# A fixed table of engine sequences, x[128] as a rank-1 term on VectorE, and GpSimd sums, in a Fourier and two-layer feed-forward kernel

## The chip, the cores and the metric

The kernel runs on one core of a Trainium2 chip. The metric is the device time of one execution in microseconds (us). A core has five engines that matter here: TensorE (PE in the profile, matrix products into the PSUM banks), VectorE (DVE), ScalarE (ACT), GpSimd (POOL) and SyncE (SP, which issues most DMA transfers). Each engine executes its own instructions strictly in the order in which they stand in its program, and waits at an instruction until the semaphores that it needs have been raised.

## What the kernel computes

The reference takes the real part of a two-dimensional Fourier transform and feeds it through two feed-forward layers:

```python
X = np.fft.fft(np.fft.fft(x, axis=1), axis=2).real       # x: 2 x 3008 x 256
x = X.reshape(6016, 256)
r = np.maximum(x @ w_in, 0.0)                             # layer 1: 256 -> 2048 -> 256
x = (r * r) @ w_out
h = x @ w_in2                                             # layer 2: 256 -> 2048 -> 256
P = a[0] + a[1]*h + a[2]*h*h + a[3]*h*h*h
Q = 1.0 + abs(b[0])*abs(h) + abs(b[1])*h*h
out = (P / (Q + 1e-6)) @ w_out2
```

The products need float32 accuracy. Each operand is therefore split into a rounded high part and a low rest, and a product is three matmuls: high by high, low by high and high by low.

## The kernel before, in words

The 6016 tokens are cut into 12 tiles: tile 0 has 384 tokens, tiles 1 to 11 have 512 (`TILES`, in units of 128). The 2048 hidden features are 16 chunks of 128. The Fourier transform along the sequence is done once for all tokens at the start (`u_mm`, `u_copy`, `u_out`, into `U`), and U for tiles 2 to 11 is spilled to DRAM. The transform along the 256 columns is done tile by tile: `fm` (matmuls, `f_d`), `fv` (copy on ScalarE), `fs` (matmuls, `f_s`), `fe` and `ff` (high and low part, `x1h` and `x1l`). The same tile's two halves of tokens are mirror images, so that from tile 2 on (tiles that are not in `DIRECT`) layer 1 multiplies an even and an odd half of 256 columns each, and gets the tokens as sum and difference of the two products.

Layer 1 on one chunk of such a tile is this chain of operations: `h1` on PE (`h1_mm`, into one PSUM bank); `b1` on ACT, which copies the odd half to SBUF; `s1` and `s2` on DVE, sum and difference into the 512-column buffer `g` (`e1_s`); `r1`, `a1`, `i1` on ACT (relu, square rounded, square); `c1` on POOL (the low part, `e1_lo`); `o1` on PE (6 matmuls of 512 columns). There are 160 such chunks (10 tiles by 16). Column 128 of the transformed input, x[128], belongs to neither half; `h1` adds it with a seventh matmul per chunk, whose stationary operand is the weight row `w0` in an otherwise empty 128 by 128 matrix and whose moving operand is `X0`, the rows that `q_row` loads from `qdram`.

Layer 2 runs on 23 subtiles: tile 0, and two of 256 tokens for each other tile. A group (two chunks of a 256-token subtile, 512 columns; one chunk of 384 in tile 0) is: `h2` (PE, 12 matmuls of 256 columns); `u` = |b1||h| and `t1` on ACT; `q` = (u + |b0|) h, `t2` and `t3` on DVE; `w` = |q|, `y` and `z` on ACT (z is 1/Q); `gh`, `m`, `e` on DVE; `c2` on POOL (`e2_gl`); `o2` on PE (12 matmuls of 256 columns). So there are 16 groups in a 512-token tile. The last two subtiles have another form (`ALONE`: `gh` on POOL; `FIN`: two single chunks).

The order of every engine is made when the program is built. `Queues.run` is a list scheduler: it holds a cost for every operation and a `place`, and takes again and again the operation that can start earliest, ties by place; `SHIFT` moves places of groups of operations. Buffers are counted in `SLOTS` (a buffer, such as `g` with two, is taken by one operation and given back by a later one), and so are the PSUM banks: `p0` to `p3`, `o1a`, `o1b`, `o2a`, `o2b`. Before, `h1` and `h2` take one of p0, p1, p2, o2b, and `m` writes p3. Loads and stores stand in one queue on SP, in program order; a store of output waits there for its ACT copy.

The lines that matter: L743 (`h1`'s matmuls) and L745 (the seventh), L769 (`o1`, `o2`), L713 (`h2`), L788 (`s1`, `s2`), L813 (`c1`), L842 (`q`), L850 (`t2`), L854 (`t3`), L876 (`gh`), L882 (`m`), L889 (`e`), L893 (`c2`), L911 and L912 (output).

Of the kernel before, what the change touches and what calls it, by code (L numbers as in the profile page):

```python
# [9 lines left out]
F32 = mybir.dt.float32  # L10
# [20 lines left out]
SLOTS = dict(xt=4, x1h=2, x1l=2, x0=2, x2h=2, x2l=2, ut=1, v=2, g=2, bc=2, g1=2, u=4, t1=4, y=3, g2=3, os=1,  # L31
# [36 lines left out]


def ranks(key):  # L70

# [41 lines left out]
}


class Queues:
# [19 lines left out]
    def run(self):  # L136
        waits, users = {}, {}
# [6 lines left out]
        ready = {}  # L144
        for op in self.ops:
            ready.setdefault(op["engine"], [])
            if not waits[op["n"]]:
                ready[op["engine"]].append(op)
        clock = dict.fromkeys(ready, 0.0)
        order = []  # L150
        while any(ready.values()):
            best = None
            for e, ops in ready.items():
                now = clock[e]
                for op in ops:
                    start = max(now, op["at"], self.port if op["port"] else 0.0)
                    for tag in op["take"]:
                        at = self.first(tag)[0]
                        if at is None:
                            break  # L160
                        start = max(start, at)
                    else:
                        rank = (start, op["place"], op["n"])
                        if best is None or rank < best[0]:
                            best = rank, op
            (start, _, _), op = best
# [5 lines left out]
            end = start + op["cost"]  # L172
# [954 lines left out]
```

## Time and profile before

| | |
|---|---|
| median of three runs | 1049.68 us (1049.3 to 1049.74) |
| the profiled execution | 1048.59 us |
| its span, first to last instruction | 1046.6 us |
| mean granted TensorE clock | 0.998 |
| PE, PEld busy | 1021.6 us (98%), 968.4 us (93%) |
| DVE, ACT, POOL busy | 998.0 us (95%), 955.6 us (91%), 495.0 us (47%) |
| matmuls | 7538 |

PEld is the loading of weights into the array, beside the matmuls. An instruction's duration in the profile runs to the end of its last write, and the next instruction of the same engine may start before that; so the time that an instruction takes of its engine is better read from the distance of two starts than from its duration, and the busy time of PE, DVE and ACT is an upper bound of their work.

### The profile page before, as it was taken

Reading aid. Unit: us, or ns where it says so; the run is one execution under the profiler, and the core shown is the slowest. Engines: PE = TensorE matmul, PEld = TensorE weight load, DVE = VectorE, ACT = ScalarE, POOL = GpSimd, SP = SyncE. Lnnn points to the kernel's source line nnn. Section 1 sums busy time; section 2 is a strip of 40 time slices with the busy share of each in tenths; the row PEclk is TensorE's granted clock in tenths of the full one; section 3 lists DMA queues with packets and bytes.
Section 4 is the critical chain, followed back from the end, with each engine's and each line's share of the span. In section 5 each row is a group of like instructions: output and inputs, shape, how many; then the busy total and the mean of one; then the engine's idle time right before and its main releaser. Section 6 shows DMA issues by size and latency. Waiting matters only on the chain.

```text
span 1046.6 us, 20738 instructions
## 1 busy us (share of the span) xinstructions
PE 1021.6 (98%) x7538; PEld 968.4 (93%) x7538; DVE 998.0 (95%) x1789; ACT 955.6 (91%) x1921; POOL 495.0 (47%) x373
## 2 busy tenths in 40 slices
PE   9899989999999999999999999999999999999986
PEld 9889989999999999999999999999999999999985
DVE  6999999999999999999999799999999999999998
ACT  3688989999998999999999899999899989999896
POOL 0000026545555555455555645655564545555476
PEclk9999999999999999999999999999999999999999
DMA  9653500000000000000000000000000000000000
GB/s 350 215 204 111 169 1 1 9 19 12 11 12 11 12 19 3 12 11 12 11 12 11 1 11 22 1 12 16 16 11 11 2 11 12 2 11 11 1 12 21
DMA packets 26939, 36.90 MB, mean 35 GB/s; under 512 B 2349, under 2 KB 19445, under 8 KB 26837
## 3 DMA queue, kind: packets, MB, share of 16 engines
q1 hardware_dynamic: 26725, 35.19, 9.9%
q8 instruction: 59, 0.97, 0.4%
q14 instruction: 43, 0.35, 0.1%
q10 hardware_dynamic: 112, 0.39, 0.1%
HBM read 26.74 MB, written 8.80 MB: 34 GB/s over the span
## 4 chain that ended last, share of the span: by engine, by line
PE 76%; DVE 9%; ACT 9%; DMA 3%; issue 2%; POOL 1%; POOLq 0%; SPq 0%; ACTq 0%; DVEq 0%
PE o2a L769 20%; PE p L713 15%; PE o1a L769 10%; PE o1b L769 10%; PE p L743 8%; PE o2b L713 5%; PE o2b L743 2%; PE p L745 1%; DMA g<-in_dram 1%; DVE g L876 1%; DMA xt<-in_dram 1%; PE o2b L769 1%; DVE p L882 1%; ACT t L836 1%; DVE t L854 1%
## 5 line engine op out<-in xcount | busy, mean ns | idle before, releaser
L893 POOL TENSOR_TENSOR g<-t,y 128x512 fp32r<-128x512 f32 (+1 forms) x182 | 250.5, 1376 | 248.7 <-DVE t L889 182.2
L813 POOL TENSOR_TENSOR g<-g,g 128x512 fp32r<-128x512 f32 x160 | 216.3, 1353 | 285.9 <-ACT g L808 237.0
L769 PE MATMUL o2a<-g,w2hi 128*128 128x256 f32 (+1 forms) x1440 | 258.7, 280 | 6.3 <-POOL g L893 6.3
L769 PEld LDWEIGHTS o2a<-g,w2hi 128*128 128x128 f32 x1440 | 209.2, 188 | 12.6 <-POOL g L893 7.9
L769 PE MATMUL o2a<-g,w2lo 128*128 128x256 f32 (+1 forms) x720 | 143.6, 279 | 0.0
L876 DVE SCALAR_TENSOR_TENSOR g<-t,ab,y 128x512 fp32r<-128x512 f32 (+1 forms) x176 | 136.8, 780 | 4.6 <-ACT y L863 2.8
L769 PE MATMUL o1a<-g,w1hi 128*128 128x512 f32 x352 | 139.5, 396 | 0.0
L769 PE MATMUL o1b<-g,w1hi 128*128 128x512 f32 x352 | 138.3, 393 | 0.0
L882 DVE SCALAR_TENSOR_TENSOR p<-u,g 128x512 f32<-128x512 f32 (+1 forms) x176 | 132.0, 750 | 0.1
L889 DVE SCALAR_TENSOR_TENSOR t<-t,ab,p 128x512 f32<-128x512 f32 (+1 forms) x176 | 127.5, 724 | 0.3
L863 ACT ACTIVATE y<-y 128x512 f32<-128x512 f32 (+1 forms) x185 | 117.8, 637 | 1.2
L713 PE MATMUL p<-x2h,w2hi 128*128 128x256 f32 (+1 forms) x540 | 109.7, 284 | 7.3 <-DVE x1h L887 2.5
L846 ACT ACTIVATE u<-u 128x512 f32<-128x512 f32 (+1 forms) x176 | 110.3, 628 | 6.5 <-DVE u L842 6.1
L788 DVE TENSOR_TENSOR g<-p,bc 128x256 f32<-128x256 f32 x260 | 106.0, 414 | 9.7 <-POOL g L813 7.6
L804 ACT ACTIVATE g<-g 128x512 fp32r<-128x512 f32 (+1 forms) x175 | 110.1, 630 | 5.1 <-PE o1b L769 4.5
L798 ACT ACTIVATE g<-g 128x512 f32<-128x512 f32 x160 | 101.8, 637 | 13.7 <-DVE g L788 13.2
L859 ACT ACTIVATE y<-u 128x512 f32<-128x512 f32 (+1 forms) x176 | 110.9, 631 | 1.9
L808 ACT ACTIVATE g<-g 128x512 f32<-128x512 f32 (+1 forms) x175 | 110.2, 631 | 1.0
L769 PEld LDWEIGHTS o2a<-g,w2lo 128*128 128x128 f32 x720 | 109.8, 188 | 0.0
L713 PE MATMUL p<-x2h,w2lo 128*128 128x256 f32 (+1 forms) x540 | 108.3, 282 | 0.0
L713 PE MATMUL p<-x2l,w2hi 128*128 128x256 f32 (+1 forms) x540 | 108.1, 282 | 0.0
L842 DVE SCALAR_TENSOR_TENSOR u<-u,ab,p 128x512 f32<-128x512 f32 (+1 forms) x134 | 96.8, 723 | 6.1 <-ACT t L836 5.5
(265 smaller groups left out, 2768.4 us busy)
## 6 DMA issues: line engine op xcount, KB each, us to landing
g<-in_dram SPq DMA_DIRECT2D x48, 256.0 KB
xt<-in_dram SPq DMA_DIRECT2D x15, 384.0 KB
out_dram<-os SPq DMA_DIRECT2D x22, 256.0 KB
udram<-U SPq DMA_DIRECT2D x4, 640.0 KB
ut<-udram SPq DMA_DIRECT2D x10, 256.0 KB
x2h<-in_dram SPq DMA_DIRECT2D x8, 256.0 KB
x2l<-in_dram SPq DMA_DIRECT2D x8, 256.0 KB
x<-qdram SPq DMA_DIRECT2D x30, 1.0 KB
```

The lines of the kernel that those rows point to most:

```text
L713: nc.tensor.matmul(h[:, c * n:(c + 1) * n], l[:, k, :], r[:, k], start=(q == 0), stop=(q == 5))
L769: nc.tensor.matmul(O[t][e], l[:, e * 128:(e + 1) * 128], r[:, c * n:(c + 1) * n], start=(i == 0 and q == 0 and (e == 0 or not one)), stop= ...
L804: nc.scalar.activation(out=e["gh"], in_=e["g"], func=ACTF.Square)
L808: nc.scalar.activation(out=e["g"], in_=e["g"], func=ACTF.Square)
L813: eng.tensor_tensor(out=e["gl"], in0=e["g"], in1=f32(e["gh"]), op=ALU.subtract)
L846: nc.scalar.activation(out=w, in_=w, func=ACTF.Abs)
L859: nc.scalar.activation(out=e["z"], in_=e["w"], func=ACTF.Abs_reciprocal_sqrt, bias=Q1)
L863: nc.scalar.activation(out=z, in_=z, func=ACTF.Square)
L876: nc.vector.scalar_tensor_tensor(out=e["gh"], in0=e["t1"], scalar=a0, in1=e["z"], op0=ALU.add, op1=ALU.mult)
L882: nc.vector.scalar_tensor_tensor(out=e["m"], in0=e["w"], scalar=Q1, in1=f32(e["gh"]), op0=ALU.add, op1=ALU.mult)
L889: nc.vector.scalar_tensor_tensor(out=e["t1"], in0=e["t1"], scalar=a0, in1=e["m"], op0=ALU.add, op1=ALU.subtract)
L893: (nc.vector if (t, j) in FIN else nc.gpsimd).tensor_tensor(out=e["gl"], in0=e["t1"], in1=e["z"], op=ALU.mult)
```

## The change

It has three parts. First, `SHIFT` and the `place` of each operation go; a table `ORDER` gives each of the five engines its whole sequence, and `Queues.run` only deals out buffers and banks in that order. With it `bc` has 3 buffers, `u` and `t1` 5, `y` 4, and p3 joins the banks of `h1` and `h2`.

Second, in tiles 2 to 11 the seventh matmul goes. x[128] now stands in row 64 of the odd half (`q_row`, now step `fq`: two DMA rows into `x1h` and `x1l` after `ff`), so that the sum `s1` holds it; the difference needs a correction, which `s2` adds as `beta` (a weight column per chunk) times `X0` (a row that `q_wide` broadcasts to all partitions) in one scalar_tensor_tensor on DVE, and POOL subtracts the odd half in a new step `s3`. The zeroing, placing and rounding of the 128 by 2048 matrix `w0` go, and the load of w_in's row moves behind the first 16 weight chunks.

Third, for groups in `SUMS` (j % 4 == 1: 40 groups of 512 columns and 4 of 384) the sum |b0||h| + |b1|h² is no longer made on DVE by `q`: ACT makes |b0||h| (`u`) and the square (`v`), and POOL adds them (`w`). In the other groups `q` writes into the h2 bank, and so does `m` (p3 is no longer needed); `t3` of `SUMS` writes into the bank instead. There `m` takes its first operand from SBUF, and in the others from the bank.

```diff
-SLOTS = dict(xt=4, x1h=2, x1l=2, x0=2, x2h=2, x2l=2, ut=1, v=2, g=2, bc=2, g1=2, u=4, t1=4, y=3, g2=3, os=1,
+SLOTS = dict(xt=4, x1h=2, x1l=2, x0=2, x2h=2, x2l=2, ut=1, v=2, g=2, bc=3, g1=2, u=5, t1=5, y=4, g2=3, os=1,
...
-BANKS5 = BANKS + ("o2b",)
+BANKS5 = BANKS + ("o2b", "p3")
...
+ORDER = dict(
+    SP=
+    "040I06050J08070K090A0L0B0C0M03000N010O0P020Q0R0S0T0U0V0o0W0X0H0p0Y0D0F0E0Z0G0z0a1J0b0c0d0e0f0g0h0i0j"
...
+        for e, text in ORDER.items():
+            place = [62 * DIGITS.index(a) + DIGITS.index(b) for a, b in zip(text[::2], text[1::2])]
...
+    SUMS = [(t, j) for t in range(M) for j in range(len(GROUPS2[t])) if (t, j) not in ALONE + FIN and j % 4 == 1]
...
+    def q_wide(t):
+        X0[t] = x0t[t % 2]
+        nc.sync.dma_start(out=X0[t], in_=q_part(t, 2).partition_broadcast(128))
+
     def q_row(t):
...
+        for part in range(2):
+            nc.sync.dma_start(out=f32(X1[t][part][64:65, 1, :]), in_=q_part(t, part).unsqueeze(0))
...
+            if k == jobs[-1] and t not in DIRECT:
+                add(("fq", t), "SP", 0.2, lambda t=t: q_row(t), needs=["qd"] + [("ff", t, i) for i in jobs], lat=DMA_LAT)
...
-            for b in range(2):
-                for q, (l, r) in enumerate(((wh, xh), (wl, xh), (wh, xl))):
-                    nc.tensor.matmul(h[:, b, c], l[:, b, :], r[:, b, :n], start=(q == 0), stop=(b == 1 and q == 2))
-                if b == 0:
-                    nc.tensor.matmul(h[:, 0, c], w0[:, i], X0[t][:, :n], start=False, stop=True)
+            for q, (l, r) in enumerate(((wh, xh), (wl, xh), (wh, xl))):
+                for b in range(2):
+                    nc.tensor.matmul(h[:, b, c], l[:, b, :], r[:, b, :n], start=(c + q + b == 0), stop=(c == gs - 1 and q == 2 and b == 1))
...
+        if part == 0:
+            nc.vector.tensor_tensor(out=g[:, 0], in0=H1[t, j][:, 0, 0], in1=b, op=ALU.add)
+        elif part == 1:
+            i = GROUPS1[t][j][0]
+            nc.vector.scalar_tensor_tensor(out=g[:, 1], in0=X0[t], scalar=beta[:, i:i + 1], in1=H1.pop((t, j))[:, 0, 0],
+                                           op0=ALU.mult, op1=ALU.add)
+        else:
+            nc.gpsimd.tensor_tensor(out=g[:, 1], in0=g[:, 1], in1=b, op=ALU.subtract)
...
+    def e2_v(t, j):
+        e = E2[t, j]
+        e["z"] = sb(tag2("y", t, j), [128, NMAX])[:, :e["n"]]
+        nc.scalar.activation(out=e["z"], in_=H2[t, j], func=ACTF.Square, scale=SCALES[3])
+
+    def e2_vw(t, j):
+        e = E2[t, j]
+        nc.gpsimd.tensor_tensor(out=e["w"], in0=e["w"], in1=e["z"], op=ALU.add)
...
-        e["w"] = H2[t, j] if (t, j) in ALONE + FIN else w
+        e["w"] = H2[t, j]
         nc.vector.scalar_tensor_tensor(out=e["w"], in0=w, scalar=b0, in1=H2[t, j], op0=ALU.add, op1=ALU.mult)
...
+        e["t3"] = H2[t, j] if (t, j) in SUMS else e["t1"]
+        nc.vector.scalar_tensor_tensor(out=e["t3"], in0=e["t1"], scalar=a1, in1=H2[t, j], op0=ALU.add, op1=ALU.mult)
...
-        e["m"] = e["w"] if (t, j) in ALONE + FIN else ps(tag2("m", t, j), [128, NMAX])[:, :e["n"]]
+        e["m"] = e["w"]
         nc.vector.scalar_tensor_tensor(out=e["m"], in0=e["w"], scalar=Q1, in1=f32(e["gh"]), op0=ALU.add, op1=ALU.mult)
```

Three places show what that makes of the programs. On TensorE, this is a chunk of `h1` of tile 7 before (p_7580 is its bank, x1h and x1l the two parts of its input, w_73 the matrix with the row of x[128]):

```order
L743 MATMUL p_7580<-x1h,w1hi_78 128x256
L743 MATMUL p_7580<-x1h,w1lo_94 128x256
L743 MATMUL p_7580<-x1l,w1hi_78 128x256
L745 MATMUL p_7580<-x_75,w_73 128x256
L743 MATMUL p_7580<-x1h,w1hi_78 128x256
L743 MATMUL p_7580<-x1h,w1lo_94 128x256
L743 MATMUL p_7580<-x1l,w1hi_78 128x256
```

In the changed kernel the same step reads as follows, and the six matmuls of `o1` of an earlier chunk come behind it:

```order
L788 MATMUL p_7483<-x1h,w1hi_78 128x256 x2
L788 MATMUL p_7483<-x1h,w1lo_94 128x256 x2
L788 MATMUL p_7483<-x1l,w1hi_78 128x256 x2
L812 MATMUL o1a<-g_7417,w1hi_91 128x512
L812 MATMUL o1b<-g_7417,w1hi_91 128x512
```

Seven matmuls have become six; the even and the odd half alternate, and nothing that needs `X0` is left on TensorE.

On VectorE, in the middle of tile 6, these are consecutive instructions before (u, t and y are the layer-2 buffers, p_ and o2b are banks, g<-p,bc is `s1` or `s2`):

```order
L788 TENSOR_TENSOR g<-p_7082,bc 128x256
L882 SCALAR_TENSOR_TENSOR p_7129<-u,g_7091 128x512
L854 SCALAR_TENSOR_TENSOR t_7039<-t_7039,ab,p_7006 128x512
L889 SCALAR_TENSOR_TENSOR t_7019<-t_7019,ab,p_7129 128x512
L788 TENSOR_TENSOR g<-p_7082,bc 128x256
L842 SCALAR_TENSOR_TENSOR u<-u,ab,o2b 128x512
L850 TENSOR_TENSOR t_7134<-t_7134,o2b 128x512
L842 SCALAR_TENSOR_TENSOR u<-u,ab,p_7112 128x512
L850 TENSOR_TENSOR t_7170<-t_7170,p_7112 128x512
L876 SCALAR_TENSOR_TENSOR g_7185<-t_7039,ab,y 128x512
```

And these in the changed kernel, where L833 is the new `s2`, L936 `gh`, L942 `m`, L951 `e`, L898 `q`, L908 and L913 `t2` and `t3`:

```order
L908 TENSOR_TENSOR t_6715<-t_6715,p_6634 128x512
L913 SCALAR_TENSOR_TENSOR p_6634<-t_6715,ab,p_6634 128x512
L830 TENSOR_TENSOR g<-p_6679,bc 128x256
L833 SCALAR_TENSOR_TENSOR g<-x_74,beta,p_6679 128x256
L936 SCALAR_TENSOR_TENSOR g_6772<-t_6676,ab,y 128x512
L942 SCALAR_TENSOR_TENSOR p_6592<-p_6592,g_6772 128x512
L908 TENSOR_TENSOR t_6777<-t_6777,p_6737 128x512
L951 SCALAR_TENSOR_TENSOR t_6676<-t_6676,ab,p_6592 128x512
L913 SCALAR_TENSOR_TENSOR t_6777<-t_6777,ab,p_6737 128x512
L898 SCALAR_TENSOR_TENSOR p_6737<-u,ab,p_6737 128x512
```

The group whose bank is p_6634 is one of `SUMS`: it has no `q`, and its `t3` lands in the bank. In the other two `m` reads and writes the bank; before, it read the buffer u in SBUF.

On SyncE, these are consecutive instructions of the middle tiles before (x_74 and x_75 are the two `X0` buffers, ut is the next tile's U):

```order
L634 DMA x_74<-qdram 1x256 x3
L542 DMA ut<-udram 128x2x256
L912 DMA out_dram<-os 128x2x256 x2
L542 DMA ut<-udram 128x2x256
L634 DMA x_75<-qdram 1x256 x3
```

And these in the changed kernel, where L681 is `fq`, L677 the broadcast and L974 the output:

```order
L974 DMA out_dram<-os 128x2x256
L582 DMA ut<-udram 128x2x256
L677 DMA x_74<-qdram 128x256
L974 DMA out_dram<-os 128x2x256
L681 DMA x1h<-qdram 1x256
L681 DMA x1l<-qdram 1x256
```

`X0` was loaded as three rows at any time before its tile; now there is one broadcast, and two rows that come only after the tile's `ff` and stand behind output stores in the same queue.

## Rows read from the trace of the kernel before

**Rows 1.** The page, busy time, share of the span and instructions of four engines.

```profile
PE 1021.6 (98%) x7538; PEld 968.4 (93%) x7538; DVE 998.0 (95%) x1789; ACT 955.6 (91%) x1921; POOL 495.0 (47%) x373
```

**Rows 2.** Busy time by stretch: PE, PEld, DVE, ACT, POOL (instructions), clock, DMA share, GB/s.

```profile
0.00:60.00 60.00, 53.82 (x393) 50.82 (x394) 47.09 (x126) 33.16 (x82) 2.51 (x7) 1.00 0.75 264
60.00:110.00 50.00, 49.85 (x357) 47.55 (x356) 47.42 (x104) 44.17 (x92) 0.00 (x0) 1.00 0.47 164
110.00:200.00 90.00, 86.54 (x511) 80.25 (x511) 87.96 (x180) 83.91 (x184) 31.28 (x26) 0.98 0.12 39
200.00:960.00 760.00, 758.87 (x5710) 721.02 (x5709) 735.47 (x1253) 718.78 (x1423) 407.89 (x300) 1.00 0.04 11
960.00:1046.60 86.60, 72.56 (x575) 68.79 (x573) 80.08 (x131) 75.58 (x144) 53.36 (x41) 1.00 0.03 10
```

**Rows 3.** Line L745, the seventh matmul: duration in ns min/median/max, first and last start.

```profile
L745 PE MATMUL p<-x,w x130: 278/281/290, 131.7 to 971.7; 128*128 128x256 f32 x130
L745 PE MATMUL o2b<-x,w x30: 279/281/290, 252.3 to 966.8; 128*128 128x256 f32 x30
```

**Rows 4.** Timeline of TensorE: start, duration (us), operation, count.

```profile
501.57 0.29 PE L745 MATMUL p<-x,w 128*128 128x256 f32 x1
...
502.05 0.40 PE L769 MATMUL o1a<-g,w1hi 128*128 128x512 f32 x1
502.29 0.39 PE L769 MATMUL o1b<-g,w1hi 128*128 128x512 f32 x1
...
509.16 0.28 PE L745 MATMUL p<-x,w 128*128 128x256 f32 x1
...
509.62 0.40 PE L769 MATMUL o2a<-g,w2hi 128*128 128x256 f32 x2
```

**Rows 5.** Groups of VectorE, shapes apart: count, busy us, mean ns, idle before.

```profile
L876 DVE SCALAR_TENSOR_TENSOR g<-t,ab,y 128x512 fp32r<-128x512 f32 x160 | 126.6, 794 | 3.5 <-ACT y L863 2.8 <-DVE g L876 0.2
L882 DVE SCALAR_TENSOR_TENSOR p<-u,g 128x512 f32<-128x512 f32 x160 | 122.6, 766 | 0.0
...
L882 DVE SCALAR_TENSOR_TENSOR p<-p,g 128x512 f32<-128x512 f32 x9 | 6.3, 695 | 0.3
```

**Rows 6.** Timeline of VectorE in the middle: start, duration (us).

```profile
640.06 1.33 DVE L876 SCALAR_TENSOR_TENSOR g<-t,ab,y 128x512 fp32r<-128x512 f32 x1
641.32 0.74 DVE L842 SCALAR_TENSOR_TENSOR u<-u,ab,o2b 128x512 f32<-128x512 f32 x1
641.98 0.69 DVE L882 SCALAR_TENSOR_TENSOR p<-u,g 128x512 f32<-128x512 f32 x1
642.58 0.75 DVE L876 SCALAR_TENSOR_TENSOR g<-t,ab,y 128x512 fp32r<-128x512 f32 x1
...
648.33 0.42 DVE L788 TENSOR_TENSOR g<-p,bc 128x256 f32<-128x256 f32 x1
648.66 0.41 DVE L788 TENSOR_TENSOR g<-o2b,bc 128x256 f32<-128x256 f32 x1
```

**Rows 7.** Timeline of GpSimd just before the first row of rows 6.

```profile
639.54 1.31 POOL L893 TENSOR_TENSOR g<-t,y 128x512 fp32r<-128x512 f32 x1
```

**Rows 8.** Groups of GpSimd, shapes apart: count, busy us, mean ns, idle before.

```profile
L893 POOL TENSOR_TENSOR g<-t,y 128x512 fp32r<-128x512 f32 x166 | 233.1, 1404 | 228.8 <-DVE t L889 171.9 <-ACT g L798 7.5 <-ACT y L863 7.1
...
L893 POOL TENSOR_TENSOR g<-t,y 128x384 fp32r<-128x384 f32 x16 | 17.4, 1090 | 20.0 <-DVE t L889 10.2 <-ACT g L798 3.2 <-PE p L713 2.8
```

**Rows 9.** Timeline at the end: a 256-column operation of VectorE, the last copy.

```profile
1036.24 0.47 DVE L854 SCALAR_TENSOR_TENSOR t<-t,ab,o1b 128x256 f32<-128x256 f32 x1
...
1043.05 0.60 ACT L911 ACTIVATE os<-o2a 128x512 f32<-128x512 f32 x1 [4.33 <-PE o2a L769]
```

**Rows 10.** Waits of TensorE and VectorE: total us, times, longest.

```profile
PE o2a L769 <- POOL g L893: 6.3, 8, 1.5
...
DVE g L788 <- POOL g L813: 8.6, 12, 2.5
```

More of the change, by code (lines that the diff above doesn't have):

```diff
@@ L143, in run @@
                 users.setdefault(x["n"], []).append((op, late))
[L144 to L149, printed above, removed]
+            lines.setdefault(op["engine"], []).append(op)
+        for e, text in ORDER.items():
+            place = [62 * DIGITS.index(a) + DIGITS.index(b) for a, b in zip(text[::2], text[1::2])]
+            assert sorted(place) == list(range(len(lines[e])))
+            lines[e] = [lines[e][i] for i in place]
+        clock, done = dict.fromkeys(lines, 0.0), dict.fromkeys(lines, 0)
         order = []
-        while any(ready.values()):
+        while len(order) < len(self.ops):
             best = None
[L153 to L166, printed above, removed]
+            for e, line in lines.items():
+                op = line[done[e]] if done[e] < len(line) else None
+                if op is None or waits[op["n"]]:
+                    continue
+                ats = [self.first(tag)[0] for tag in op["take"]]
+                if None not in ats:
+                    at = max([clock[e], op["at"]] + ats)
+                    if best is None or at < best[0]:
+                        best = at, e, op
+            start, e, op = best
             for tag in op["take"]:
@@ L181, in run @@
                 waits[x["n"]] -= 1
[L182 to L187 removed]
+            order.append(op["fn"])
+        return order
 def act(n, psum=False, ptr=0):
@@ L934, in body @@
             o1 = o1_tag(t)
-            add(("h1",) + key, "PE", (7 if t not in DIRECT else 12) * gs * mm(EN[t]), place, f(h1_mm),
-                needs=[k for k in queues.by_key if k[0] in ("ff", "fn", "q") and k[1] == t] + ["w0"] * (t not in DIRECT) + [("W", 1, i) for i in chunks],
-                take=(one_of("h1", t, j),), give=("x1h", "x1l", "y" if t in DIRECT else "x0") if end else (), lat=0.2,
+            add(("h1",) + key, "PE", (6 if t not in DIRECT else 12) * gs * mm(EN[t]), f(h1_mm),
+                needs=[k for k in queues.by_key if k[0] in ("ff", "fn", "fq") and k[1] == t] + [("W", 1, i) for i in chunks],
+                take=(one_of("h1", t, j),), give=("x1h", "x1l") + ("y",) * (t in DIRECT) if end else (), lat=0.2,
@@ L985, in body @@
-            add(("t2",) + key, "DVE", dve(n), place, f(e2_t2), needs=[("t1",) + key])
-            add(("t3",) + key, "DVE", dve(n, ptr=1), place, f(e2_t3), needs=[("t2",) + key],
-                after=[] if inbank else [("q",) + key], give=() if inbank else held)
-            add(("w",) + key, "ACT", act(n, inbank), place, f(e2_w), needs=[("q",) + key])
-            add(("y",) + key, "ACT", act(n, inbank), place, f(e2_y), needs=[("w",) + key], take=(one_of("y", t, j),),
-                after=chain("y", BEFORE2, key))
@@ L991, in body @@
-            add(("z",) + key, "ACT", act(n), place, f(e2_z), needs=[("y",) + key])
+            sums = key in SUMS
+            chained = chain("y", BEFORE2, key)
+            free, held, half = given("u", t, j), given("h2", t, j), given("t1", t, j)
+            if sums:
+                add(("v",) + key, "ACT", act(n, True), f(e2_v), needs=[("u",) + key], take=(one_of("y", t, j),), after=chained)
+                add(("w",) + key, "POOL", pool_tt(n), f(e2_w), needs=[("v",) + key])
+            else:
+                add(("q",) + key, "DVE", dve(n, ptr=1), f(e2_q), needs=[("u",) + key, ("t1",) + key],
+                    after=[("t3",) + key], give=(free,))
+                add(("w",) + key, "ACT", act(n), f(e2_w), needs=[("q",) + key])
@@ new lines, in body @@
+            add(("t2",) + key, "DVE", dve(n), f(e2_t2), needs=[("t1",) + key])
+            add(("t3",) + key, "DVE", dve(n, ptr=1), f(e2_t3), needs=[("t2",) + key],
+                after=[("v",) + key] if sums else [], give=(half,) if sums else ())
+            add(("y",) + key, "ACT", act(n, not sums), f(e2_y), needs=[("w",) + key],
+                take=() if sums else (one_of("y", t, j),), after=[] if sums else chained)
+            add(("z",) + key, "ACT", act(n), f(e2_z), needs=[("y",) + key])
@@ L992, in body @@
             if alone:
-                add(("P",) + key, "ACT", act(n, ptr=1), place, f(e2_p), needs=[("t3",) + key])
+                add(("P",) + key, "ACT", act(n, ptr=1), f(e2_p), needs=[("t3",) + key])
             gh = ("POOL", pool_tt(n)) if alone else ("DVE", dve(n, ptr=1))
-            add(("gh",) + key, *gh, place, f(e2_gh), needs=[("z",) + key, ("P" if alone else "t3",) + key],
-                take=(one_of("g2", t, j),), after=chain("gh", BEFORE2, key), port=True)
-            add(("m",) + key, "DVE", dve(n), place, f(e2_m), needs=[("gh",) + key], port=not inbank,
-                take=() if inbank else (one_of("m", t, j),), give=() if inbank else free)
@@ L999, in body @@
-            add(("e",) + key, "DVE", dve(n, ptr=0 if alone else 1), place, f(e2_e), needs=[("m",) + key], give=held if inbank else (given("m", t, j),))
-            add(("c2",) + key, *(("DVE", dve(n)) if fin else ("POOL", pool_tt(n))), place, f(e2_gl), needs=[("e",) + key], port=True,
-                give=(given("t1", t, j), given("y", t, j)))
-            add(("o2",) + key, "PE", pe, place + (gs - 1) * step + (LAG2 if t < M - 1 else LAG_END), fg(mm_o, G2, W2, O2, "o2"),
+            add(("gh",) + key, *gh, f(e2_gh), needs=[("z",) + key, ("P" if alone else "t3",) + key],
+                take=(one_of("g2", t, j),), after=chain("gh", BEFORE2, key), port=not sums)
@@ L1003, in body @@
+            add(("m",) + key, "DVE", dve(n), f(e2_m), needs=[("gh",) + key], port=sums)
+            add(("e",) + key, "DVE", dve(n, ptr=0 if alone else 1), f(e2_e), needs=[("m",) + key], give=(held,))
+            add(("c2",) + key, *(("DVE", dve(n)) if fin else ("POOL", pool_tt(n))), f(e2_gl), needs=[("e",) + key], port=True,
+                give=(free if sums else half, given("y", t, j)))
+            add(("o2",) + key, "PE", pe, fg(mm_o, G2, W2, O2, "o2"),
                 needs=[("c2",) + key] + [("W", 2, i) for i in chunks], take=() if j else ("o2a",) if t else ("o2a", "o2b"),
```

414 lines of the change are left out of this document (232 added, 182 removed), and 21 rows, old and new, of the table SHIFT.

## The prediction

> **What bounds the kernel now.** The page comes first: TensorE is busy 98% of the span, VectorE 95%, ScalarE 91%, GpSimd 47% [rows 1]. Two engines close to full cannot both be the bound everywhere, so the second view is the busy time by stretch [rows 2]. From 200 to 960 us TensorE is idle 1.1 us of 760, while VectorE is idle 24.5. In that stretch a microsecond of TensorE's work is a microsecond of the span. TensorE's other idle time, 25.0 us in all, is 6.2 us in the first 60, 3.5 us from 110 to 200, and 14.0 us from 960 on. The last of these holds the way out: the last copy starts 3.55 us before the end of the span [rows 9], which leaves 10.5 us of waits in the last stretch. There and from 110 to 200 VectorE is busy 80.1 of 86.6 us and 88.0 of 90 [rows 2], so those waits, 14 us together, are waits for a loaded VectorE and what hangs on it; the longest item of TensorE's list of waits is `c2` on GpSimd with 6.3 us [rows 10]. Weight loads (PEld) run beside the matmuls, one each, and go with them.
>
> **The seventh matmul goes: -18.8 us.** L745 ran 130 times into a p bank and 30 times into o2b, 160 in all [rows 3]. Its duration of 281 ns is no price, since matmuls overlap. The timeline gives the pace: from one L745 to the matmul behind the three that follow it are 0.48 us, in another chunk 0.46 us, for four matmuls each [rows 4], so 0.1175 us for one. 160 x 0.1175 = 18.8 us, with 18.4 and 19.2 as ends. All of them lie between 131.7 and 971.7 us [rows 3], mostly in the stretch where TensorE has no idle time. So this counts in full if the others keep up.
>
> **Can VectorE keep up?** Distances of starts give its prices: 0.66 us for a 512-column operation with a pointer scalar (`q`, `t3`, `gh`, `e`), 0.60 for `m` (and I take `t2` alike), 0.33 for `s1` [rows 6]. A 512-token tile costs 16 x (4 x 0.66 + 2 x 0.60) = 61.4, plus 32 x 0.33 = 10.6, plus about 1.9 for the low parts (two 256-column and two 512-column operations): 73.9 us. TensorE needs 16 x 7 x 0.1175 = 13.2 for `h1`, 96 x 0.24 = 23.0 for `o1` [rows 4], 384 x 0.115 = 44.2 for `h2` and `o2`: 80.4. I take 80 for the tile's period, so VectorE has 6 us of slack. After the change four of 16 `q` go (-2.6), and `s2` becomes an operation with a pointer. The trace has no such `s2`; the nearest is the 256-column `t3` at the end, 0.47 us long where the plain 256-column operation is 0.41 to 0.42 [rows 9, 6]. So +0.06 each, +1.0 per tile (ends: 0, and +0.33 if a pointer form needed twice the time, +5.3 per tile, which would eat the slack). VectorE: 72.3 of a period of 80 - 16 x 0.1175 = 78.1, slack 5.8. The two engines shrink alike, and the cover stays.
>
> **VectorE against GpSimd.** Two VectorE operations take both inputs from SBUF: `gh` and `m` of most groups. At 640.06 a `gh` takes 1.33 us instead of 0.75 [rows 6]; a GpSimd instruction ran from 639.54 to 640.85 [rows 7], and `gh` ended 0.54 us behind it. `gh` averages 794 ns, and `m` 766 where its first input is in SBUF, against 695 from a bank [rows 5]. That is 0.05 and 0.07 us per operation, 19 us for 320. The Trainium skill, page "SBUF — State Buffer", section "Who interferes with whom", says that a VectorE instruction with two SBUF inputs and a GpSimd instruction that reads SBUF exclude each other for the whole length of the one that started first. The trace agrees, with this 1.33 us. The change works on both sides of this. `m` of 132 groups goes into the bank (-9.2 us), `gh` of 44 reads a bank (-2.2 us); 132 `gh` and 44 `m` still collide. GpSimd gets more work: 44 sums at 1.40 us, and 160 `s3` of 256 columns. The trace has no `s3`; between 512 columns at 1404 ns and 384 at 1090 [rows 8] lie 2.45 ns per column, so 0.78 us (ends 0.70, half the 512, and 1.09, the 384). GpSimd's 495 us grow by 125 + 60 to some 680, and in the middle from 54% [rows 2] to (42.9 + 16 x 0.78 + 4 x 1.40) / 78.1 = 78% of a tile. If collisions grow with that share, 176 x 0.06 x 0.44 = +4.7 us.
>
> VectorE's total: 44 `q` less, -28.5 (four are narrower); `s2` +9.6; collisions -9.2 - 2.2 + 4.7. Sum -25.6 us, where TensorE loses 18.8. The surplus of 6.8 us can only be earned where TensorE waits for VectorE, the 14 us above. The last groups (`ALONE`) keep their `q`, so not all of it is to be had: I take 4 us (ends 0 and 14, the latter if the new sequences removed every such wait).
>
> **What I cost at nothing.** ScalarE makes 44 `v` in place of 44 `w` and loses the rounding of `w0`; at 719 of 760 us [rows 2] it lies under TensorE, and one operation per chunk more would be seen. The three DMA rows per tile become one broadcast and two rows, the rows on the path from `ff` to `h1`, in SP's queue behind stores that wait for ScalarE. Their cover is TensorE's other work between a tile's last `fs` and its first `h1`; without it each tile would pay at most what the last store takes, 1046.6 - 1043.65 = 2.95 us [rows 2, 9], so 0 to 30 us; I take 0, since only the first `h1` of a tile waits. `s3` puts GpSimd into the layer-1 chain, 0.78 us plus a wait of up to one instruction (1.40) ahead of it; the cover is the second `g` buffer. The banks: `m` in the h2 bank holds it longer, and p3 joins for that. The start (6.2 us of TensorE idle) I leave as it is.
>
> **Sum.** 1048.59 (the profiled execution, 2.0 over its span) - 18.8 - 4 = 1025.8; the median of the runs lies 1.1 above that execution, so **1027 us**.
>
> **The rivals.** *VectorE loses at GpSimd's door (slower).* Each contender in the middle tiles (12 `gh` and 4 `m` per tile) loses time to a GpSimd that is busy 78%. Slack is 5.8 us per tile, so nothing is seen up to 0.36 us per contender, six times today's 0.06. One that is hit loses 0.58 (1.33 - 0.75, [rows 6]). If all are hit: 9.3 - 5.8 = 3.5 us per tile, 35 us over ten tiles, 1062 us; it turns slower than before from 0.51 us each. If 78% are hit: 0.45 each, 14 us, 1041. For it: GpSimd's share. Against: half as many contenders, and today's GpSimd at 54% costs 0.06, not 54% of 0.58. The skill's page "Perfetto Trace Analysis", section "Optimizing Scalar/DVE Operations", warns that moving work between VectorE and GpSimd might not help because they share a port; by that the 44 sums would bring nothing and the time would be 1031, TensorE's 18.8 us alone.
>
> *The layer-1 chain becomes the wait.* Today VectorE waits 12 times, 8.6 us, for `c1` to give `g` back [rows 10], 0.7 us each. Two buffers leave 9.8 us per chunk pair. If the longer chain made every chunk wait 0.45 us, 7.2 - 5.8 = 1.4 us per tile would come out, 14 in all: 1041.
>
> *The sequences win the waits too.* All 14 us of TensorE's waits for VectorE go: 1049.7 - 18.8 - 14 = 1017.
>
> *TensorE is not the bound.* Then its freed time turns into idle time and VectorE's -25.6 decides: 1024, hardly apart from the forecast. Only if VectorE's relief fails as well does nothing come of it: 1050.
>
> **Chances.** Forecast (1019 to 1035) 0.70; 1019 or lower 0.10; the GpSimd or chain rival with 1035 to 1047 0.12; slower 0.06; no change 0.02. A change under 0.2% (2.1 us) is about what a measurement of this kernel cannot tell from none. Faster 0.92, same 0.02, slower 0.06. The range of 1017 to 1041 leaves out some 2 in 10: the lower end is all waits won, the upper one of the partial rivals.
>
> **What would show it.** Right: no L745 and 160 matmuls less; TensorE without idle time in the middle and the first layer-2 tiles some 2 us shorter each; `s2` near 0.47 us; `m` near 0.69 in the 132 groups; `s3` near 0.78; GpSimd near 680 us. Wrong: `gh` well over 0.9 us on average, TensorE waiting for `g` through `s1` or for `x1h` after a DMA, a middle stretch with TensorE idle by 2 us per tile, or a last stretch longer than 86.6 us.

## The result, and the profile after

The changed kernel takes 1037.63 us (median of four runs, 1037.38 to 1039.1) against 1049.71 (1049.3 to 1051.9) for the kernel before: a ratio of 0.9884 (95% interval 0.9866 to 0.9901), 12.1 us faster. The forecast of 1027 us lay 10.6 us too low, inside its range. The profiled execution took 1039.1 us, its span is 1037.3.

The page of the changed kernel, as in [rows 1]:

```profile
PE 1007.3 (97%) x7378; PEld 949.8 (92%) x7378; DVE 980.5 (95%) x1754; ACT 955.1 (92%) x1922; POOL 668.2 (64%) x574
```

160 matmuls are gone, VectorE is busy 17.5 us less, GpSimd 173 us more. Its stretches, as in [rows 2]:

```profile
0.00:60.00 60.00, 53.06 (x376) 51.09 (x376) 45.04 (x123) 30.65 (x79) 0.20 (x4) 0.94 0.75 257
60.00:110.00 50.00, 49.05 (x352) 46.82 (x353) 49.15 (x115) 42.88 (x92) 0.00 (x0) 1.00 0.53 169
110.00:200.00 90.00, 84.24 (x497) 75.31 (x496) 87.75 (x173) 81.77 (x176) 37.74 (x35) 1.00 0.13 41
200.00:960.00 760.00, 756.33 (x5636) 714.91 (x5635) 726.46 (x1228) 733.02 (x1452) 579.61 (x497) 1.00 0.04 13
960.00:1037.30 77.30, 64.66 (x523) 61.65 (x521) 72.13 (x120) 66.79 (x129) 50.60 (x39) 1.00 0.03 11
```

Most of the gain is made ahead of 960 us: the last stretch begins with less left and is 9.3 us shorter, of which 1.4 us are idle time of TensorE (12.6 us, 14.0 before). But TensorE's idle time is 3.7 us in the middle (1.1 before), 5.8 from 110 to 200 (3.5 before), 6.9 in the first 60 (6.2 before). In this execution the granted clock fell to its lower level, 1.2 GHz, behind 1.6 us of idle time at the start:

```profile
30.00:35.00 5.00, 3.44 (x26) 3.03 (x24) 3.29 (x9) 2.21 (x7) 0.00 (x0) 1.00 1.05 361
35.00:40.00 5.00, 4.28 (x21) 4.30 (x21) 4.62 (x15) 2.79 (x8) 0.00 (x0) 0.50 0.97 329
```

New prices, in the view of groups with shapes apart:

```profile
L936 DVE SCALAR_TENSOR_TENSOR g<-t,ab,y 128x512 fp32r<-128x512 f32 x120 | 100.7, 840 | 3.2 <-ACT y L923 1.6 <-PE o2a L812 1.0
L942 DVE SCALAR_TENSOR_TENSOR p<-p,g 128x512 f32<-128x512 f32 x105 | 72.5, 694 | 1.0 <-POOL g L934 0.3
L951 DVE SCALAR_TENSOR_TENSOR t<-t,ab,p 128x512 f32<-128x512 f32 x97 | 72.0, 744 | 1.2
L833 DVE SCALAR_TENSOR_TENSOR g<-x,beta,p 128x256 f32<-128x256 f32 x139 | 65.8, 473 | 0.0
...
L836 POOL TENSOR_TENSOR g<-g,bc 128x256 f32<-128x256 f32 x160 | 133.5, 835 | 196.6 <-ACT g L851 143.0 <-DVE g L833 39.0 <-ACT t L892 4.1
```

`s2` takes 473 ns (0.47 was the estimate), `s3` 835 (0.78, within its ends), `m` in the bank 694, `gh` with both inputs in SBUF 840 where it was 794 [rows 5]. And the list of TensorE's waits from 110 to 285 us (total us, times, longest):

```profile
PE p L758 <- DVE u L951: 2.0, 3, 1.0
PE p L758 <- DVE t L951: 1.6, 2, 0.9
PE p L618 <- DVE t L951: 1.6, 2, 1.0
```

L951 is `e`, which gives the bank of `h2` back. In the kernel before `t3` (L854) gave it back, and the waits of that name came to 2.3 us in this stretch:

```profile
PE p L713 <- DVE t L854: 2.3, 2, 1.3
```

### The profile page after: what moved, and what is told of

The parts are those of the page before. It is cut to its first block, busy times and chain, and to the rows that moved or that the text cites. A ratio compares the mean times of both kernels' runs of the same rounds, so it can differ in the third digit from the quotient of the medians.

```text
span 1037.3 us, 20505 instructions
## 1 busy us (share of the span) xinstructions
PE 1007.3 (97%) x7378; PEld 949.8 (92%) x7378; DVE 980.5 (95%) x1754; ACT 955.1 (92%) x1922; POOL 668.2 (64%) x574
## 4 chain that ended last, share of the span: by engine, by line
PE 75%; ACT 10%; DVE 9%; DMA 3%; issue 2%; POOL 0%; SPq 0%; POOLq 0%; DVEq 0%; ACTq 0%
PE o2a L812 19%; PE p L758 15%; PE o1a L812 10%; PE o1b L812 10%; PE p L788 8%; PE o2b L758 4%; PE p L771 1%; PE o2b L788 1%; PE p L773 1%; DVE g L936 1%; DMA xt<-in_dram 1%; ACT t L892 1%; DVE t L908 1%; DMA g<-in_dram 1%; ACT u L878 1%
## 5 line engine op out<-in xcount | busy, mean ns | idle before, releaser
L836 POOL TENSOR_TENSOR g<-g,bc 128x256 f32<-128x256 f32 x160 | 133.5, 835 | 196.6 <-ACT g L851 143.0
L955 POOL TENSOR_TENSOR g<-t,y 128x512 fp32r<-128x512 f32 (+1 forms) x139 | 188.3, 1357 | 41.6 <-DVE t L951 24.7
L758 PE MATMUL p<-x2h,w2hi 128*128 128x256 f32 (+1 forms) x568 | 115.9, 285 | 7.2 <-DVE t L951 3.2
L923 ACT ACTIVATE y<-y 128x512 f32<-128x512 f32 (+2 forms) x187 | 117.5, 630 | 1.4
L936 DVE SCALAR_TENSOR_TENSOR g<-t,ab,y 128x512 fp32r<-128x512 f32 (+2 forms) x133 | 108.8, 819 | 3.3 <-ACT y L923 1.6
L908 DVE TENSOR_TENSOR t<-t,p 128x512 f32<-128x512 f32 (+1 forms) x150 | 100.1, 668 | 8.0 <-ACT t L892 5.2
L758 PEld LDWEIGHTS p<-x2h,w2hi 128*128 128x128 f32 x568 | 89.5, 188 | 16.3 <-DVE t L951 4.6
L892 ACT ACTIVATE t<-p,ab 128x512 f32<-128x512 f32 (+1 forms) x150 | 102.4, 683 | 0.0
L878 ACT ACTIVATE u<-p 128x512 f32<-128x512 f32 (+1 forms) x148 | 86.7, 586 | 5.7 <-PE p L758 5.0
L758 PEld LDWEIGHTS p<-x2l,w2hi 128*128 128x128 f32 x568 | 87.1, 188 | 0.9 <-DVE x2l L871 0.9
```

What stands on the lines that cost most here:

```text
L758: nc.tensor.matmul(h[:, c * n:(c + 1) * n], l[:, k, :], r[:, k], start=(q == 0), stop=(q == 5))
L836: nc.gpsimd.tensor_tensor(out=g[:, 1], in0=g[:, 1], in1=b, op=ALU.subtract)
L892: nc.scalar.activation(out=e["t1"], in_=H2[t, j], func=ACTF.Identity, scale=SCALES[0], bias=a2)
L908: nc.vector.tensor_tensor(out=t1, in0=t1, in1=H2[t, j], op=ALU.mult)
L923: nc.scalar.activation(out=z, in_=z, func=ACTF.Square)
L936: nc.vector.scalar_tensor_tensor(out=e["gh"], in0=e["t3"], scalar=a0, in1=e["z"], op0=ALU.add, op1=ALU.mult)
```

## The experiments

**Which part of the 12 us is the matmul's?** One matmul is put back in front of each chunk of `h1` in the changed kernel, and in the other direction the seventh is taken out of the kernel before.

```diff
# seventh_back (in the changed kernel)
+            nc.tensor.matmul(h[:, 0, c], wl[:, 0, :], xh[:, 0, :n], start=True, stop=True)
             for q, (l, r) in enumerate(((wh, xh), (wl, xh), (wh, xl))):
# before_no_seventh (in the kernel before)
-                if b == 0:
-                    nc.tensor.matmul(h[:, 0, c], w0[:, i], X0[t][:, :n], start=False, stop=True)
```

> The changed kernel with one more matmul of 256 columns ahead of the six in each of the 160 h1 chunks of tiles 2 to 11 (its result is overwritten by the next matmul, the output is unchanged). Theory A, the price of the prediction was right and TensorE is the bound in the middle: 160 x 0.1175 = 18.8 us, of which the 32 chunks of tiles 2 and 3 (3.8 us) may lie in TensorE's waits there, so 1037.6 + 15 to 18.8 = 1053 to 1056 us. Rival, the saved time was turned into waits for VectorE in the middle as well: at most 6 us more, 1044 or less.

> The kernel before, its own order kept, with the seventh matmul left out and nothing in its place (the output lacks x[128] in tiles 2 to 11); VectorE has all its work. Theory A, VectorE's 6 us of slack per tile cover it: 1049.7 - 18.8 = 1031 us, up to 1035 if the first two tiles give nothing. Rival, VectorE without relief is the pace as soon as TensorE gets shorter: 1042 or more, with TensorE idle in the middle stretch by 1 us or more per tile.

seventh_back: 1053.91 us, ratio to before 1.0048 (1.0034 to 1.0063). From 0.9884 to 1.0048 are 17.2 us: the 18.8 of the forecast, within the intervals. But it also says that all the rest of the change makes the kernel 5.0 us slower (3.6 to 6.6), where the forecast had it 4 us faster. seventh_back has as many matmuls as the kernel before, 7538, so the counts show where it falls behind:

```profile
0.00:60.00 60.00, 54.17 (x397) 51.80 (x398) 47.58 (x130) 32.05 (x82) 0.20 (x4) 1.00 0.75 262
60.00:110.00 50.00, 49.29 (x355) 47.05 (x355) 49.06 (x113) 44.05 (x93) 0.00 (x0) 1.00 0.54 178
110.00:200.00 90.00, 83.69 (x496) 75.27 (x495) 88.67 (x172) 82.25 (x177) 39.35 (x37) 1.00 0.10 33
200.00:285.00 85.00, 84.43 (x628) 79.81 (x627) 79.28 (x135) 80.19 (x160) 63.60 (x55) 1.00 0.06 18
285.00:960.00 675.00, 674.50 (x5063) 640.27 (x5063) 637.01 (x1069) 641.33 (x1265) 503.73 (x433) 1.00 0.04 12
```

The kernel before makes 393, 357, 511, 651 and 5062 matmuls in these stretches. So 38 are lost from 110 to 285 us and none earlier; at 0.148 us each (171.5 busy us for 1162 in the kernel before) that is 5.6 us. From 285 to 960 us the two keep pace, and behind 960 us some of it comes back, since TensorE is idle 12.6 us there instead of 14.0:

```profile
960.00:1049.40 89.40, 76.77 (x610) 73.01 (x608) 83.76 (x139) 78.58 (x151) 59.23 (x46) 0.99 0.04 13
```

The profiled execution of seventh_back was the fastest of its four, 1051.22 us, 2.6 us above that of the kernel before (1048.59). So the trace accounts for 2.6 us; where the medians get the rest of the 5.0 us from, no trace shows.

before_no_seventh: 1040.61 us, ratio 0.9919 (0.9904 to 0.9933): 8.5 us, under half of 18.8 and between the two expectations. Its middle stretch, and behind it that of the kernel before:

```profile
285.00:960.00 675.00, 672.92 (x4978) 634.56 (x4977) 656.03 (x1118) 641.94 (x1274) 366.17 (x270) 1.00 0.03 11
```

```profile
285.00:960.00 675.00, 673.87 (x5062) 639.79 (x5061) 650.60 (x1107) 637.71 (x1263) 363.79 (x268) 1.00 0.03 11
```

The page counts TensorE as busy in both, yet the matmuls come every 135.6 ns (675 us / 4978). Before, 675 us less 131 seventh matmuls of 0.1175 us leave 133.8 ns for each of the others; at that pace 67 more would fit in, 9.0 us. In this order they do not close ranks when one is taken out. The edited loop of `h1` is not where it is lost: from start to start, a matmul of `h2` takes 117.2 ns on average in this stretch where it took 115.4, and a 256-column one of `o2` 117.7 where it took 115.6, with their code unchanged.

**Is it VectorE's load that holds the other half?** The same kernel also without the 44 `q`:

```diff
# before_both (in before_no_seventh)
+        if (t, j) not in ALONE + FIN and j % 4 == 1:
+            return
         nc.vector.scalar_tensor_tensor(out=e["w"], in0=w, scalar=b0, in1=H2[t, j], op0=ALU.add, op1=ALU.mult)
```

> The kernel before in its own order without the seventh matmul and without q in the 44 groups that the change gives to GpSimd (w reads u; both parts of the output are left out), so that VectorE loses 44 x 0.66 = 28 us and nothing is put in their place. This is the prediction's sum without the costs of s2, s3, the banks and the new sequences. If the sum was right (18.8 and 4): 1027 us. If VectorE's relief only lets the matmuls' 18.8 us count: 1031. If the 10 us that before_no_seventh lost are not VectorE's load: 1037 to 1041.

1039.77 us, ratio 0.9912 (0.9897 to 0.9927). VectorE's busy time falls by 16.0 us, from 996.9 to 980.9, and not by 28, since more of `gh` and `m` now meet GpSimd (818 and 798 ns on average, 797 and 769 in before_no_seventh). This relief brings nothing that can be told from zero (0.8 us, the intervals overlap). In the middle VectorE falls from 656.0 to 643.5 us, and TensorE still makes 4978 matmuls; behind 960 us TensorE is idle 13.5 us, 13.6 without the relief. So the half that was lost is not VectorE's load. The order of the engines is the suspect that is left, but no run changes the order alone.

**The stretch from 110 to 285 us.** VectorE is busy 87.75 of 90 us there, so its load was the first suspect. Two kernels take work off it.

```diff
# w2_short (in the changed kernel)
     def w_b3(j):
+        raw = RW.pop(j)
+        if j >= NF:
+            return
# w2_low_on_gpsimd: w_lo of W2
-        nc.vector.tensor_tensor(out=w["lo"][i][:, cols], in0=x, ...
+        (nc.vector if m == 1 else nc.gpsimd).tensor_tensor(out=w["lo"][i][:, cols], in0=x, ...
```

> The changed kernel without the last decoding step of W2 (the 16 operations that put the low bits in, 512 columns each, 87 to 142 us; W2 loses these bits). VectorE gets 16 x 0.69 = 11 us less there, with nothing moved to GpSimd. Theory C, VectorE paces the stretch up to 285 us, where TensorE's idle time grew by 6 us: most of the 11 us show, 1028 to 1033 us. Rival D2, the new sequences as such or the clock at the start make that idle time: 1035 to 1038.

> The changed kernel with the 16 low parts of W2 (512 columns, SBUF to SBUF, 87 to 142 us) on GpSimd, which is idle up to 140 us, instead of VectorE; on GpSimd each stands where it stood in time. Theory C, VectorE is the pace from 110 to 285 us: it loses 16 x 0.6 = 9.6 us there, of which the 6 us that TensorE waits more than before come back, 1030 to 1033. If GpSimd's SBUF reads cost VectorE as much as they take off it: 1037 to 1040. Theory B, the banks: not over 2 us, 1036 to 1038.

w2_short: 1038.34 us, ratio 0.9899 (0.9884 to 0.9914), no gain. VectorE is busy 7.9 us less in all (972.7 us). It has 4.9 us of idle time from 110 to 200 us, and TensorE waits as before (L954 is `e` here):

```profile
110.00:200.00 90.00, 84.40 (x502) 76.11 (x501) 85.15 (x166) 82.52 (x178) 38.29 (x36) 1.00 0.12 39
...
PE p L761 <- DVE u L954: 1.9, 2, 1.0
PE p L621 <- DVE t L954: 1.6, 2, 1.0
PE p L761 <- DVE t L954: 1.5, 2, 0.9
```

Theory C, VectorE as the pace of this stretch, falls. w2_low_on_gpsimd: 1044.97 us, ratio 0.9955 (0.9943 to 0.9968), 7 us slower than the changed kernel. Its decoding operations from 87 to 142 us:

```profile
L474 DVE SCALAR_TENSOR_TENSOR cw<-g,cw 128x512 uint32<-128x512 uint32 x14 | 14.8, 1060 | 0.1
...
L464 DVE TENSOR_SCALAR cw<-cw 128x512 uint32<-128x512 uint32 x15 | 9.1, 609 | 0.2
```

In the changed kernel these take 685 and 423 ns in the same window. VectorE is busy 987.1 us, 6.6 more than in the changed kernel, although 11.0 us were taken off it.

**The bank.** The view of TensorE's waits names `e`. A group of tile 0 shows why; this is `u`, the first reader of the bank, and `e` of the fourth group in the changed kernel's timeline, then `u` and `t3`, which gave the bank back, in that of the kernel before:

```profile
146.73 0.55 ACT L878 ACTIVATE u<-p 128x384 f32<-128x384 f32 x1
...
157.49 0.61 DVE L951 SCALAR_TENSOR_TENSOR t<-t,ab,p 128x384 f32<-128x384 f32 x1
```

```profile
143.38 0.57 ACT L831 ACTIVATE u<-p 128x384 f32<-128x384 f32 x1
...
146.90 0.60 DVE L854 SCALAR_TENSOR_TENSOR t<-t,ab,p 128x384 f32<-128x384 f32 x1
```

From `u`'s start the bank is held for 11.4 us, before for 4.1. Over the 16 groups of tile 0 these distances of rows average 9.8 and 5.7 us, over those of tile 1 13.0 and 8.2. Against it stands one bank more: four instead of three in tile 0, five instead of four later. To test it, the bank was given back early again, in two ways; both keep `q` in SBUF, and m_in_p3 moves a few entries of `ORDER`.

```diff
# m_in_p3: q in u, m in p3, h2 bank given back by q; p3 is no bank of h1 and h2
-BANKS5 = BANKS + ("o2b", "p3")
+BANKS5 = BANKS + ("o2b",)
-        e["m"] = e["w"]
+        e["m"] = e["w"] if (t, j) in ALONE + FIN + SUMS else ps("p3", [128, NMAX])[:, :e["n"]]
# m_in_sbuf: q and m in u, all five banks kept; m_in_sbuf_early: range(6) for range(M)
+    SOON = [(t, j) for t in range(M) for j in range(len(GROUPS2[t])) if (t, j) not in ALONE + FIN + SUMS]
-        e["w"] = H2[t, j]
+        e["w"] = w if (t, j) in SOON else H2[t, j]
```

> The changed kernel with m of the 132 groups whose denominator is not GpSimd's back in the p3 bank and q back in SBUF, so that the h2 bank is given back by q and not only by e; p3 is no bank of h1 and h2 any more. Theory B, the h2 banks are what TensorE waits for from 110 to 285 us (waits named after the e line, 5 us): these go, VectorE pays 132 x 0.07 = 9 us of collisions in its slack, 1031 to 1034 us. Rival C, VectorE itself is the pace there (88 of 90 us busy): the waits only change their name and the collisions add 1 to 4 us, 1038 to 1042.

> The changed kernel, its sequences and its five banks kept, but q and m of the 132 groups whose denominator is not GpSimd's stay in the u buffer (SBUF), so that the h2 bank is given back behind q and not behind e; the u buffer is held until e instead. Theory B, the bank held longer is what TensorE waits for from 110 to 285 us: the 5 us of waits named after the e line go there, 1032 to 1033 us. Against it, m and gh of 132 groups collide with GpSimd again, 132 x 0.07 = 9 us of VectorE, which lie in its slack of about 23 us from 285 to 960. Rival C, VectorE is the pace from 110 to 285 us: no gain there, 1037 to 1042.

> The same edit in the first six layer-2 tiles only (up to about 340 us), the rest as in the changed kernel. Theory B: the same 1032 to 1033 us, with no collisions behind. Rival C: 1037 to 1039.

m_in_p3: 1149.9 us, ratio 1.097 (1.0934 to 1.1006). m_in_sbuf: 1142.35, 1.0873 (1.0851 to 1.0896). m_in_sbuf_early: 1068.57, 1.0186 (1.017 to 1.0202). All expectations missed, by up to 108 us. Groups of VectorE with shapes apart, m_in_sbuf (`m` and `e`), then m_in_p3 (`m`):

```profile
L943 DVE SCALAR_TENSOR_TENSOR u<-u,g 128x512 f32<-128x512 f32 x160 | 157.5, 986 | 1.3
L952 DVE SCALAR_TENSOR_TENSOR t<-t,ab,u 128x512 f32<-128x512 f32 x120 | 144.2, 1203 | 1.5
```

```profile
L942 DVE SCALAR_TENSOR_TENSOR p<-u,g 128x512 f32<-128x512 f32 x120 | 124.3, 1036 | 1.1
```

`m` and `e` with both inputs in SBUF take 986 and 1203 ns; in the changed kernel, with one from a bank, 694 and 744. In m_in_sbuf these are 160 x 0.29 + 120 x 0.46 = 102 us, about the whole loss of 105. In m_in_p3 `m` accounts for 120 x 0.34 = 41 us of 112; what the rest is, with a bank fewer, is not shown.

This is the first rival, GpSimd's door, in full size. Two inputs in SBUF alone do not open it: the 40 `m` of `SUMS` have them in the changed kernel too, and take 698 ns. The timeline of m_in_sbuf shows what does:

```profile
644.19 1.74 POOL L888 TENSOR_TENSOR u<-u,y 128x512 f32<-128x512 f32 x1
...
644.81 1.67 DVE L952 SCALAR_TENSOR_TENSOR t<-t,ab,u 128x512 f32<-128x512 f32 x1
```

`e` starts while a GpSimd instruction runs and ends 0.55 us behind it (646.48 and 645.93). Counted over the traces, 92 of the 120 `e` of m_in_sbuf start so, on average 0.75 us before the end of that instruction, and 94 of the 160 `m`; the other `m` take 683 ns. In the changed kernel it is 9 of the 40 `m` of `SUMS`, 0.16 us before the end, and 52 of the 120 `gh`, 0.38 us. An operation with an input in a bank is not held: 72 of the 105 `m` that read a p bank start well inside a GpSimd instruction and take 694 ns, the others 693. So the price depends on where the fixed order puts an operation beside GpSimd, and m_in_sbuf puts new two-SBUF operations into an order that was made without them.

So the bank theory could not be tested alone: an earlier release by these means brings the collisions back. That the longer hold costs the 5 us is argued from the distances, the names of the waits and their staying in w2_short; it is not shown by a kernel without it. The traces also speak against the hold alone: from tile 3 to tile 10 the same distances are 13 to 15 us by tile in seventh_back and 5 to 7 in the kernel before, more than twice as long, and from 285 to 960 us, most of that time, TensorE loses no matmul. Why it loses some ahead of 285 us stays open.

**More and fewer sums, and the rank-1 term alone.**

```diff
# more_sums_early
-... and j % 4 == 1]
+... and (j % 4 == 1 or t < 3 and j % 4 == 3)]
# no_sums, rank1_alone (ORDER changed too, not shown; the latter has the order of the kernel before,
# s3 and fq put in, four banks and m in p3 as before, and the buffer counts of the change)
-    SUMS = [(t, j) for t in range(M) ...]
+    SUMS = []
```

> The changed kernel with eight more sums on GpSimd in the first three layer-2 tiles (j = 3, 7, 11, 15 as well), so that VectorE has eight q less from 130 to 290 us, some 5 us. Theory C, VectorE paces there: 1033 to 1036 us. Rivals: GpSimd's added 11 us collide with VectorE's operations or stand in front of its c2 and s3, 1038 or more; no effect, 1037 to 1038.

> The changed kernel with no sum on GpSimd: the 44 groups have q on VectorE (behind t3) and w on ScalarE (ahead of y) again, like the other groups of the change; all else as in the change. VectorE gains about 29 us, ScalarE nothing, GpSimd loses 62 us. Theory A3, the relief is what the middle needs (VectorE idle for 29 of 675 us there, unevenly): 1045 to 1060 us. Rival, the rank-1 term alone brings the gain: 1037 to 1041.

> The order of the kernel before with the rank-1 term alone: six matmuls per h1 chunk, s2 with the pointer, s3 on GpSimd put in by the time at which s2 ended before, the rows of x[128] loaded as in the change; every q on VectorE, m in p3 as before. Leaving the matmul out altogether gave 8.5 us. Theory A2, VectorE's load decides (it gains 10 us of s2 and loses nothing): the 8.5 us are gone, 1046 to 1056. Rival E, the sequences and the sums of GpSimd matter little: 1031 to 1041.

more_sums_early: 1055.3 us, 1.0063 (1.0049 to 1.0076), 18 us slower than the changed kernel, with VectorE busy 71.29 of 85 us from 200 to 285. The sum on GpSimd lengthens the way to `e`; VectorE and TensorE stand in their fixed order and wait. no_sums: 1092.31, 1.0415 (1.0395 to 1.0436). rank1_alone: 1191.74, 1.1369 (1.1344 to 1.1395), 142 us slower than before. One line of each view of waits (more_sums_early from 110 to 285 us, no_sums from 285 to 960, rank1_alone whole):

```profile
DVE p L913 <- ACT y L883: 10.3, 8, 2.8
```

```profile
ACT p L904 <- DVE p L898: 19.7, 19, 3.3
```

```profile
ACT g L845 <- POOL g L836: 153.0, 136, 4.3
```

In rank1_alone ScalarE's `r1` waits 136 times for `s3`, 1.1 us each; in the changed kernel, whose order leaves room for `s3`, that wait is 5.2 us in all. The load of VectorE alone explains none of the three. Only the rival of more_sums_early (1038 or more) held; no_sums lies 32 us above its highest expectation, and both theories of rank1_alone were too mild, since they counted work and not what stands behind a wait. All three put work into an order that was not made for it or take it out, so their times are not the price of that work alone.

**The start.** The first 45 us in the order of the kernel before:

```diff
# old_start: ORDER's beginnings on SP, ScalarE, VectorE, TensorE
-TensorE: hot0, um0_1, um0_0, um1_1, um1_0, ... fs0_0, fs0_1, qm0, fm1_0, qm5, ...
+TensorE: hot0, um0_0, um0_1, um1_0, um1_1, ... qm0, qm5, qm10, qm15, fs0_0, fs0_1, qs, ...
```

> The changed kernel with the first 45 us in the order of the kernel before on SP, ScalarE, VectorE and TensorE (the constants ahead of the first weights, the u chunks in their order); the rest in the order of the change. Theory D, the start of the new sequences costs the 3 us by which TensorE's idle time grew up to 110 us: 1034 to 1035 us. Rival C, VectorE paces from 110 to 285 us whenever TensorE arrives there: 1037 to 1038, the 3 us come back as a longer wait behind 110 us.

1042.91 us, ratio 0.9941 (0.993 to 0.9953), 5 us slower, by one wait:

```profile
PE p L618 <- ACT v L605: 4.7, 1, 4.7
```

`v` stands behind `scales` there, which in the changed kernel needs a square root from VectorE first. This tells nothing against the old order as such. seventh_back, with the new start and a full clock, makes 752 matmuls up to 110 us, the kernel before 750 [rows 2]: at a full clock the new start costs nothing that shows. In the profiled execution of the changed kernel, where the clock fell, it is 728. The mean granted clock of its four executions is 0.996 to 0.998, while that of the kernel before reaches 1.000 in some. The old order is not free of the fall either (0.89 from 30 to 60 us in before_no_seventh). So the clock at the start may hold a part of the 5.0 us, and no run tells how much.

## Why the prediction was right, and where it was off

**The seventh matmul** (-18.8): measured 17.2 in the changed kernel, with an interval that holds 18.8. But "this counts in full if the others keep up" was put on VectorE alone. In the old order only 8.5 us come of it, and VectorE's relief does not raise that. What in the changed kernel brings the other half, its sequences or something else, no run isolates. The prediction had no such condition, so that the term came out near 18.8 is in part luck.

**VectorE's relief** (-4): this is the step that failed. It was taken to shorten TensorE's 14 us of waits, because those waits are for VectorE. (The 25.0 us given for TensorE's idle time outside the middle include the middle's 1.1; nothing hangs on it.) They are waits for one operation, `t3` or `e` ahead of 285 us and mostly `c2` on GpSimd at the end, and not for a load: with VectorE busy 16 us less in before_both and 8 us less in w2_short, at most 0.8 us came of it. In the last stretch of the changed kernel 1.4 of the 14.0 us of idle time went; from 110 to 285 us there was more of it. The sign "the first layer-2 tiles some 2 us shorter each" did not come: from the first `u` of tile 0 to the first of tile 2 are 131.5 us, 129.4 before. VectorE's total was off as well: its busy time fell by 17.5 us where -25.6 stood. The rest of the change came out at +5.0 where -4 stood; with 1.6 us of the first term that is the 10.6 us by which the forecast was low.

**The banks** (costed at nothing): "`m` in the h2 bank holds it longer, and p3 joins for that". From 110 to 285 us TensorE waits 5.2 us under the name of `e`, which gives the bank back, where it waited 2.3 under that of `t3`, so nothing was too little there. That the hold, 1.7 times as long in tile 0, is the reason is argued, as said above.

**GpSimd's door** (-9.2 and -2.2, +4.7): `m` at 694 ns and `gh` at 840 are near the estimate, so in the changed kernel the rival did not come. But the prediction let the loss grow with GpSimd's share of the time. At the same share, 64%, `m` of `SUMS` loses 0.01 us in the changed kernel (698 ns against 685 for those that start beside an idle GpSimd), and `m` and `e` lose 0.29 and 0.46 in m_in_sbuf: what counts is how many start while a GpSimd instruction runs, and how long before its end.

**The chain of layer 1** (a rival, 1041): no loss in the changed kernel, 153 us of waits in rank1_alone. The second `g` buffer, which both have, was no cover by itself; the order is. **The DMA rows** (0 to 30, taken 0): no wait for them in TensorE's list. **s2, s3, GpSimd's total** (0.47, 0.78, 680): 0.473, 0.835, 668.

## What to carry to other kernels

A wait for an engine is not a wait for its load: before a relief is counted, ask whether the awaited instruction would come sooner by it, and test it by leaving work out. A buffer that is held longer has to be priced stage by stage: the same longer hold goes with more waits ahead of 285 us and with none that count behind. Work on GpSimd is cheap as long as VectorE's operations beside it take an input from a bank, or start where GpSimd pauses; and a fixed order is tuned for exactly the operations in it.

## What the runs showed of the hardware

What an operation of VectorE with two SBUF inputs loses beside GpSimd is not set by GpSimd's share of the span. At 47% `gh` lost 0.05 us [rows 5], taking its form with one input from a bank, 747 ns in the changed kernel, as the price without loss; at 64% `gh` loses 0.09 in the changed kernel, but `m` and `e` 0.29 and 0.46 in m_in_sbuf. An operation that starts while a GpSimd instruction runs ends about 0.55 us behind that instruction's end, or after its plain time where that is later: so do all 24 `gh` and 43 `m` of the kernel before that start so, all 52 `gh` of the changed kernel, and in m_in_sbuf all 92 `e` and 88 of 94 `m`. (In the other six the GpSimd instruction lasts over 1.8 us, and `m` its plain 0.68.) An operation with one SBUF input is hit too, if it runs at the fast rate: L464 takes 423 ns for 512 columns where L474, with two, takes 685, and in w2_low_on_gpsimd the three L464 that start while a GpSimd instruction runs take 1.36 us on average. The Trainium skill, page "SBUF — State Buffer", section "Who interferes with whom", names both kinds, two SBUF inputs and the modes that use a second port; the trace agrees.

The pace of TensorE's matmuls depends on the program by more than its waits: 135.6 against 133.8 ns on average from 285 to 960 us in before_no_seventh, with the page at 672.9 busy us of 675. Why stays open.
